# A two-layer attention and MLP kernel: transposes of the LayerNorm output moved from TensorE to the DMA queue, with a reordered start and a split last store

## Chip, cores and metric

The kernel runs on one core of a Trainium2 chip. The metric is device time in microseconds (us) of one execution. All executions used here were fast (within 1.5% of the fastest of the same kernel). "PE" is TensorE, "DVE" VectorE, "ACT" ScalarE, "POOL" GpSimd and "SP" the engine whose queue issues all DMAs here.

## The reference, cut to what matters

```python
# x: 1 x 2048 x 1024, bf16;  H = 32 heads of 32;  window of W = 8 keys, 2 apart;  F = 3584
x = x + attention(layernorm(x), wqkv, wo)      # q.k over 8 earlier rows, softmax, weighted sum of v, @ wo
x = x + gelu(layernorm(x) @ w1 + b1) @ w2 + b2
x = x + attention(layernorm(x), wqkv, wo)      # the same weights a second time
x = x + gelu(layernorm(x) @ w1 + b1) @ w2 + b2
```

Almost all the arithmetic is in four matrix products per layer (wqkv, wo, w1, w2). In the code, the matmuls of wqkv and w1 take both operands with D on partitions, in eight steps of 128 (for wqkv `lhsT=ws[:, kk, dl, :]`, `rhs=xnT[:, kk, :]`). A normalised tile has rows on partitions, so it is transposed before each of wqkv and w1, to bring its columns onto partitions.

## The kernel before

The 2048 rows are cut into 4 chunks of 512 rows, each of 4 tiles of 128. Two layers make 8 chunk steps. A software clock decides where the attention of a later chunk is put between the MLP matmuls of an earlier one, so that DVE works on attention while PE works on the MLP. LN1 is the LayerNorm ahead of the attention, LN2 the one ahead of the MLP. These parts are touched:

```python
def ln_units(xt):
    xnT = xtpool.tile([P, KT, C], BF, name="xnT")
    def a_unit(st):                                  # statistics and normalisation of one 128-row tile
        # ... bn_stats, bn_aggr on DVE into mv
        nc.gpsimd.tensor_scalar(out=rstd, in0=mv[:, 1:2], scalar1=EPS, scalar2=None, op0=ALU.add)
        nc.gpsimd.tensor_tensor(out=rstd, in0=rstd, in1=neghalf, op=ALU.pow)
        xn = xnpool.tile([P, D], BF, name="xn")
        last = nc.vector.tensor_scalar(out=xn, in0=xt[:, st, :], scalar1=mv[:, 0:1], scalar2=rstd, ...)
    def b_unit(st):                                  # transpose of that tile: 8 matmuls against the identity
        xn = xns.pop(st)
        for g in range(2):
            pt = psaux.tile([P, 4, P], F32, name="pa")
            for j in range(4):
                kk = g * 4 + j
                nc.tensor.matmul(pt[:, j, :], lhsT=xn[:, kk * P:(kk + 1) * P], rhs=ident, start=True, stop=True)
            nc.scalar.activation(out=xnT[:, g * 4:(g + 1) * 4, st * P:(st + 1) * P], in_=pt, func=AF.Copy)
# ...
# attention: red() = reduction of q*k products over each head, exp() = softmax,
# bc(0), bc(1) = broadcast of the weights of a head to its lanes: 8 matmuls of 32 rows each, evicted by ACT to attn4,
# pv(dl) = product with v and sum over the window, on DVE, for dl = 0..7
# ...
def store_x(i, xt):                                  # one chunk, 1 MB, in one DMA
    nc.sync.dma_start(out=dst[c * C:(c + 1) * C, :].rearrange("(t p) d -> p t d", p=P), in_=xt)
# ...
# the head: chunk 0 and the projections of chunk 1
xa[0] = ln_all(xts[0])                               # a(st), b(st) for the 4 tiles
us0 = qkv_units(0, xa.pop(0), qks[0])                # q0 k0 q1 k1 ... then v0..v7
# ...
xa[1] = sched_ln1(1, clk.t)
for u in us0[1:]: clk.run(u, T_MM)
sched_att(0, qks.pop(0), 16 * T_MM + 4.5)            # softmax of chunk 0, placed by the clock, after the v units
us1 = qkv_units(1, xa.pop(1), None)
for u in us1[:21]: clk.run(u, T_MM)
run_wo(0, r)                                         # output projection of chunk 0, its LN2
# ... then the loop over 8 chunk steps: W1 and gelu, W2, store, projections of the next chunks
```

## Time and profile before

| | before |
|---|---|
| time, median of 4 executions (lowest to highest) | 1306.25 us (1304.83 to 1306.96) |
| span of the profiled execution | 1304.7 us |
| PE busy | 1272.7 us (98%) |
| first matmul of the first MLP | 135.71 us |
| period of the loop over chunk steps | 158.1 to 158.9 us |
| from the end of the last DVE addition to the end | 5.5 us |

The first lines are from the page of the kernel before: engine totals, then 40 equal slices of the span with busy tenths and the granted PE clock in tenths, then a queue line (packets, MB, share of 16 engines), then two groups of instructions (count, busy us and mean ns, then the idle time before them and what ended it).

```profile
PE 1272.7 (98%) x8031; PEld 826.9 (63%) x8120; DVE 789.1 (60%) x829; ACT 401.7 (31%) x648; POOL 176.7 (14%) x196
...
PE   6998999999999999999999999999999999999998
...
PEclk9998999999999999999999999999999999999999
...
q1 hardware_dynamic: 186832, 201.60, 48.3%
...
L167 ACT ACTIVATE xnT<-pa 128x512 bf16<-128x512 f32 x128 | 69.2, 595 | 421.2 <-PE pa L165 421.1
...
L165 PE MATMUL pa<-ident,xn 128*128 128x128 bf16 x512 | 42.9, 224 | 14.5 <-POOL rstd L152 10.0
```

PE is full from the fifth slice to the last. What it does there must come off PE, or nothing is gained. L165 is the transpose: 512 matmuls, 64 groups of 8.

The busy time of such short matmuls overlaps (512 of 224 ns would be 114.7 us, and the line has 42.9 us), so a group's price is read from the timeline of PE in the kernel before (start us, us, engine, line, operation, count):

```profile
562.65 0.81 PE L289 MATMUL ps<-wt,o 128*128 128x512 bf16 x3
563.30 0.61 PE L165 MATMUL pa<-ident,xn 128*128 128x128 bf16 x8
563.75 3.62 PE L289 MATMUL ps<-wt,o 128*128 128x512 bf16 x15
567.20 0.61 PE L165 MATMUL pa<-ident,xn 128*128 128x128 bf16 x8
```

From the start of a group to the start of what follows is 563.75 - 563.30 = 0.45 us. The period of the loop is read from the chain that ended last, at the long W2 piece of two successive steps (start us, us, what):

```profile
524.26 30.58 PE ps L331 x280
...
682.78 30.57 PE ps L331 x280
```

The head has a gap. In the timeline of PE in the kernel before, these are the output projection after its wait, and the first matmul of the first MLP:

```profile
116.41 1.89 PE L289 MATMUL ps<-wt,o 128*128 128x512 bf16 x4 [3.94 <-DVE o L282]
...
135.71 1.02 PE L307 MATMUL ps<-xnT,wt 128*128 128x512 bf16 x3 [0.78 <-ACT xnT L167]
```

The bracket says that PE had been idle for 3.94 us until DVE delivered o, the result of pv. What the clock did then shows in the windows of the kernel before. Each line has the window, its length, busy us with counts for PE, weight loads, DVE, ACT and POOL, then the granted clock, the DMA share and GB/s:

```profile
111.67:115.08 3.41, 0.80 (x4) 0.18 (x2) 3.41 (x4) 0.00 (x0) 0.00 (x0) 1.00 0.00 0
115.08:118.50 3.42, 2.09 (x5) 0.73 (x6) 2.20 (x5) 0.00 (x0) 0.00 (x0) 0.51 0.00 0
118.50:121.90 3.40, 3.40 (x9) 1.21 (x8) 3.15 (x7) 0.00 (x0) 0.63 (x2) 0.50 0.00 0
```

PE had almost nothing to do for 3.4 us while DVE was busy throughout, and then ran at half clock for 6.8 us. The tail is read from the last DVE instruction in the timeline of the kernel before, which ends at 1299.24 of 1304.7:

```profile
1298.55 0.69 DVE L334 TENSOR_TENSOR xt<-ps,xt 128x512 bf16<-128x512 f32 x1 [5.42 <-PE ps L331]
```

### The profile page before, as it was taken

To read this page: it belongs to the slowest core of one execution; us is meant where nothing else is said; L and a number is where in the kernel's file an instruction comes from. 1 tells how busy PE (TensorE), PEld (TensorE's weight loads), DVE (VectorE), ACT (ScalarE), POOL (GpSimd) and SP (SyncE) were. 2 spreads that over 40 slices of the span, in tenths; PEclk is the share of its full clock that TensorE was granted. 3 is DMA by queue.
4 is the path that set the end of the run, shared out by engine and by line. 5 is a ranking of instruction groups with operands and counts; after the bars stand their busy time and mean duration, and the time that the engine had idled before them with its cause. 6 is when DMAs were issued, how large, how long until landed. Compare 5 with 4: busy or idle time off the path is not lost.

```text
span 1304.7 us, 18295 instructions
## 1 busy us (share of the span) xinstructions
PE 1272.7 (98%) x8031; PEld 826.9 (63%) x8120; DVE 789.1 (60%) x829; ACT 401.7 (31%) x648; POOL 176.7 (14%) x196
## 2 busy tenths in 40 slices
PE   6998999999999999999999999999999999999998
PEld 3564458664686646856478654876548765577477
DVE  5559958894916948188671886528774484843001
ACT  3341441136212362023620345203541035401310
POOL 3002200320004100042000420003200210003000
PEclk9998999999999999999999999999999999999999
DMA  9322554634555345454464445463545435544560
GB/s 296 131 74 114 184 153 134 246 114 148 135 185 195 125 159 155 145 194 170 120 163 159 164 170 167 116 210 114 203 136 170 170 107 184 146 145 157 163 165 33
DMA packets 186912, 202.77 MB, mean 155 GB/s; under 512 B 5456, under 2 KB 152912, under 8 KB 185808
## 3 DMA queue, kind: packets, MB, share of 16 engines
q1 hardware_dynamic: 186832, 201.60, 48.3%
q8 instruction: 63, 1.03, 0.3%
q14 instruction: 17, 0.14, 0.0%
HBM read 193.21 MB, written 8.39 MB: 155 GB/s over the span
## 4 chain that ended last, share of the span: by engine, by line
PE 90%; DVE 4%; DMA 4%; POOL 1%; issue 0%; ACT 0%; SPq 0%; DVEq 0%; ACTq 0%
PE ps L331 30%; PE ps L307 30%; PE ps L189 21%; PE ps L289 6%; PE pa L165 2%; DMA xmid<-xt 2%; DVE prod L279 1%; DMA wt<-in_A_wqkv_dram 1%; DMA xt<-xmid 1%; DVE prod L280 1%; DVE stats L147 1%; DVE prod L211 1%; PE lg L199 1%; DVE prod L281 0%; PE lg L269 0%
## 5 line engine op out<-in xcount | busy, mean ns | idle before, releaser
L331 PE MATMUL ps<-wt,h 128*128 128x256 bf16 x3584 | 399.5, 273 | 0.0
L307 PE MATMUL ps<-xnT,wt 128*128 128x512 bf16 x1752 | 389.3, 379 | 2.9 <-ACT xnT L167 0.8
L331 PEld LDWEIGHTS <-h 128*128 128x128 bf16 x3584 | 348.9, 98 | 42.7 <-issue 1.2
L189 PE MATMUL ps<-xnT,wt 128*128 128x512 bf16 x1503 | 336.4, 380 | 2.6 <-DMA wt<-in_A_wqkv_dram 0.7
L307 PEld LDWEIGHTS <-wt 128*128 128x128 bf16 x1792 | 173.8, 98 | 212.8 <-issue 6.6
L189 PEld LDWEIGHTS <-wt 128*128 128x128 bf16 x1536 | 218.3, 144 | 113.1 <-issue 4.7
L334 DVE TENSOR_TENSOR xt<-ps,xt 128x512 bf16<-128x512 f32 x64 | 44.1, 690 | 312.3 <-PE ps L331 312.3
L310 ACT ACTIVATE h<-ps,b1t 128x512 bf16<-128x512 f32 x224 | 152.8, 689 | 200.9 <-PE ps L307 198.7
L167 ACT ACTIVATE xnT<-pa 128x512 bf16<-128x512 f32 x128 | 69.2, 595 | 421.2 <-PE pa L165 421.1
L279 DVE TENSOR_TENSOR prod<-attn,v 128x4096 bf16<-128x4096 bf16 x64 | 143.8, 2284 | 76.0 <-ACT attn L274 76.0
L211 DVE TENSOR_TENSOR prod<-q,k 128x4096 bf16<-128x4096 bf16 x64 | 151.5, 2394 | 17.0 <-ACT k L190 17.0
L289 PE MATMUL ps<-wt,o 128*128 128x512 bf16 x496 | 116.8, 386 | 5.7 <-DVE o L282 4.9
L151 POOL TENSOR_SCALAR rstd<-mv 128x1 f32<-128x1 f32 x64 | 36.3, 567 | 600.8 <-DVE mv L149 600.0
L218 DVE TENSOR_TENSOR prod<-prod 128x4096 bf16<-128x4096 bf16 x49 | 112.0, 2286 | 0.3
L147 DVE BATCH_NORM_STATS2 stats<-xt 128x6 f32<-128x512 bf16 x128 | 84.2, 676 | 11.3 <-DMA xt<-xmid 5.6
L289 PEld LDWEIGHTS <-o 128*128 128x128 bf16 x512 | 50.0, 99 | 62.6 <-DVE o L282 6.3
L280 DVE TENSOR_TENSOR prod<-prod 128x2048 bf16<-128x2048 bf16 x64 | 75.5, 1216 | 0.0
L317 POOL TENSOR_TENSOR xt<-xt,b2bc 128x1024 bf16<-128x1024 bf16 x32 | 70.0, 2189 | 21.1 <-DVE xn L154 21.1
L190 ACT ACTIVATE q<-ps 128x512 bf16<-128x512 f32 x64 | 38.3, 599 | 78.0 <-PE ps L189 71.2
L190 ACT ACTIVATE v<-ps 128x512 bf16<-128x512 f32 x64 | 38.2, 598 | 72.0 <-PE ps L189 69.3
L190 ACT ACTIVATE k<-ps 128x512 bf16<-128x512 f32 x64 | 38.2, 598 | 69.7 <-PE ps L189 69.7
L165 PE MATMUL pa<-ident,xn 128*128 128x128 bf16 x512 | 42.9, 224 | 14.5 <-POOL rstd L152 10.0
(49 smaller groups left out, 412.9 us busy)
## 6 DMA issues: line engine op xcount, KB each, us to landing
wt<-in_B_w_dram SPq DMA_DIRECT2D x64, 1792.0 KB, 8.1
wt<-in_A_wqkv_dram SPq DMA_DIRECT2D x24, 2048.0 KB, 8.5
wt<-in_A_wo_dram SPq DMA_DIRECT2D x8, 2048.0 KB, 7.7
xmid<-xt SPq DMA_DIRECT2D x4, 1024.0 KB, 10.5
xt<-xmid SPq DMA_DIRECT2D x4, 1024.0 KB, 5.5
out_dram<-xt SPq DMA_DIRECT2D x4, 1024.0 KB, 9.7
xt<-in_A_x_dram SPq DMA_DIRECT2D x3, 1024.0 KB, 7.2
xt<-in_A_x_dram SPq DMA_DIRECT2D x4, 256.0 KB, 3.5
```

What stands on the lines that cost most here:

```text
L147: nc.vector.bn_stats(out=stats[:, hh, :], in_=xt[:, st, hh * 512:(hh + 1) * 512])
L189: nc.tensor.matmul(pt, lhsT=ws[:, kk, dl, :], rhs=xnT[:, kk, :], start=(kk == 0), stop=(kk == KT - 1))
L190: nc.scalar.activation(out=dst[:, dl, off:off + C], in_=pt, func=AF.Copy)
L211: ins = nc.vector.tensor_tensor(out=prod, in0=q8[:, dl, :].unsqueeze(1).to_broadcast([P, W, C]), in1=window(k8, dl), op=ALU.mult)
L218: nc.vector.tensor_tensor(out=self.acc, in0=self.acc, in1=prod, op=ALU.add)
L279: nc.vector.tensor_tensor(out=t, in0=attn4, in1=window(v8, dl), op=ALU.mult)
L280: nc.vector.tensor_tensor(out=t[:, 0:4, :], in0=t[:, 0:4, :], in1=t[:, 4:8, :], op=ALU.add)
L289: nc.tensor.matmul(pt, lhsT=o8[:, dl, st * P:(st + 1) * P], rhs=wt[:, dl, hf * 512:(hf + 1) * 512], start=(dl == 0), stop=(dl == 7))
L307: nc.tensor.matmul(pt, lhsT=wt[:, kk, j * P:(j + 1) * P], rhs=xnT[:, kk, :], start=(kk == 0), stop=(kk == KT - 1))
L310: nc.scalar.activation(out=h, in_=pt, func=AF.Gelu_apprx_tanh, bias=b1t[:, f:f + 1])
L317: nc.gpsimd.tensor_tensor(out=xt[:, st, :], in0=xt[:, st, :], in1=b2bc, op=ALU.add)
L331: nc.tensor.matmul(pt[:, s2, :], lhsT=hs[f][:, st * P:(st + 1) * P], rhs=wt[:, f, :], start=(f == 0), stop=(f == FT - 1))
```

## The change

The intent is fourfold: take the transposes off PE by letting the DMA queue do 56 of 64 (52 in the loop, 4 for chunk 1 in the head); start the first projection earlier and order its units so that weight loads are hidden; run the softmax of chunk 0 directly after its last reduction, with the v units over it, so that DVE starts pv earlier; and store the last chunk in four column blocks, so that only the last quarter is exposed.

```diff
-A_RED, A_EXP, A_BC0, A_BC1, A_PV, A_PVSTEP = 2.0, 8.0, 16.0, 19.5, 23.0, 4.3
+A_RED, A_EXP, A_BC0, A_BC1, A_PV, A_PVSTEP = 2.0, 8.0, 16.0, 21.0, 23.0, 4.3
@@ pools: xnpool bufs 3 -> 5, hpool bufs FT + 2 -> FT
@@ ln_units
+            if act_rstd:                                   # chunk 0 only
+                nc.scalar.activation(out=rstd, in_=mv[:, 1:2], func=AF.Sqrt, bias=epst)
+                nc.vector.reciprocal(out=rstd, in_=rstd)
+        def t_unit():
+            for st in range(ST):
+                nc.sync.dma_start_transpose(out=xnT[:, :, st * P:(st + 1) * P], in_=xns.pop(st))
@@ run_wo and sched_ln1: b(st) on PE only if on_pe, otherwise one t() for the four tiles
@@ head
+    us0 = [us0[n] for n in (0, 2, 4, 1, 6, 3, 8, 5, 10, 7, 12, 9, 14, 11, 13, 15)] + us0[16:]
-    xa[1] = sched_ln1(1, clk.t)
-    for u in us0[1:]:
+    xa[1] = sched_ln1(1, 9.0, False)
+    for u in us0[1:16]:
         clk.run(u, T_MM)
-    sched_att(0, qks.pop(0), 16 * T_MM + 4.5)
+    clk.flush()
+    red, exp, bc, pv = att_units(0, qks.pop(0))
+    red(); exp(); bc(0); bc(1)
+    for u in us0[16:]:
+        clk.run(u, T_MM)
+    for dl in range(8):
+        pv(dl)
-    run_wo(0, r)
+    run_wo(0, r, True)                                     # the first LN2 stays on PE
@@ loop
-            xa[j + 2] = sched_ln1(j + 2, clk.t + 2.0)
+            xa[j + 2] = sched_ln1(j + 2, clk.t + 2.0, False)
-            if early_wo and n == 5:
-                run_wo(j + 1, r)
+            if early_wo and n == 4:
+                run_wo(j + 1, r, False)
+            if j == N - 1 and n % 2 == 1:
+                store_cols(j, xj, n // 2)                  # 256 KB of columns after each pair of W2 units
-        store_x(j, xts.pop(j))
+        if j < N - 1:
+            store_x(j, xj)
# cut: a warm-up of POOL's power function, PE durations in the software clock, signatures
```

## The prediction

> **What bounds it now.** TensorE (PE). The page's busy table gives PE 1272.7 of 1304.7 us (98%), DVE 60%, ACT 31%; the DMA queue takes 48% of its engines' time. From 150 us to the end PE is nearly gapless (stretch table: 25.8 to 26.0 of every 26 us). Of its 32 us of idle about 21 lie before 140 us: 10 before the first matmul, about 3 in 25 to 40, 6 in 105 to 120, where the output projection waits for the last P·V products on DVE. That gap is followed by a granted clock of 0.52 and 0.80 in the stretches from 115 and 120 us, worth about 3 us more. The tail is 5.5 us: last DVE add ends at 1299.2, then the store of a 1 MB tile.

> **Removed.** 56 of 64 transpose groups of 8 matmuls leave PE for the DMA queue (instruction order: 13 chunks' LayerNorms inside the main loop, one in the head; two stay on PE). A group holds PE for 0.45 us (timeline 563.30 to 563.75). 52 x 0.45 = 23.4 us in the loop, plus about 1.5 us of interruptions (0.3 us waiting for xn, four-matmul pieces inside W2). All of it is critical: the loop period 158.2 us (chain of waits, W2 at 524.26 and 682.78) should fall to 154 to 155. The 112 ACT evictions that go (67 us) gain nothing.

> **Head.** Softmax of chunk 0 now runs right after the last head reduction, with 44 V matmuls (about 9.7 us) over it, so the attention weights should be in place near 68 us instead of 82.4. The 34.2 us of P·V on DVE then end near 102, when PE, at its 0.219 us per matmul, just arrives at the output projection (about 103). The projection should end near 118.5 instead of 128.5, without the clock drop: 10 us, one transposed chunk included. The square root on ACT saves about 1 us before the first projection; three q tiles first hide the wait for k weights (landed 18.2).

> **Tail.** The last store shrinks to a quarter: about 2.5 us.

> **Added.** 56 DMA transposes of 256 KB, 14.7 MB on 202.8. [...] Results are needed 25 us or more after their inputs are ready, and the three-deep weight ring leaves a 8.1 us load some 16 us of slack (12.1 us per piece), so even 5 us each should hide. The sync queue is in order: a transpose waiting for xn delays weight loads behind it. In the issue order four LN1 transposes stand before the fourth W1 load; xn should be ready before that load's buffer is.

> **Sum.** 23.4 + 1.5 + 10 + 2.5 = 37 us: 1269 us, range 1257 to 1288. Faster by over 2% 0.80, within 2% 0.15, slower 0.05.

> **Right if:** transposing matmuls fall from 512 to 64; loop period near 154.5; PE gapless over 100 to 120 us at full clock; projection of chunk 0 starting near 103; PE busy near 1247.

> **Wrong if:** transposes take over 5 us, or fill the DMA engines, or block the sync queue: then W1 or xnT waits "<-DMA" appear on PE, at the fourth W1 piece or the first W1 matmul of a chunk, and DVE waits for a free xn buffer. Or if the head becomes bound by DVE (27 us of products and LN1 against 27 us of PE), with PE waiting for reductions near 50 us.

## The result, and the profile after

| | before | after |
|---|---|---|
| time, median (lowest to highest) | 1306.8 us (1304.68 to 1309.49, 13 executions) | 1266.84 us (1264.85 to 1268.38, 8 executions) |
| ratio, 95% interval | | 0.9693 (0.9684 to 0.9703) |
| profiled span | 1304.7 us | 1267.0 us |
| PE busy | 1272.7 us | 1244.5 us |
| first matmul of the first MLP | 135.71 us | 127.43 us |
| period of the loop | 158.1 to 158.9 us | 154.03 us |
| tail after the last DVE addition | 5.5 us | 3.1 us |

A ratio here is the mean time of one kernel's fast runs over that of the other's in the same rounds, so it is not quite the ratio of the medians that are quoted. The difference of 3.1% makes it faster. All outputs agreed with the reference.

The lines of the page after that answer to those shown of before:

```profile
PE 1244.5 (98%) x7589; PEld 803.2 (63%) x7672; DVE 786.3 (62%) x834; ACT 344.8 (27%) x541; POOL 151.6 (12%) x190
...
PEclk9989999999999999999999999999999999999999
...
q1 hardware_dynamic: 247552, 216.29, 57.8%
```

The transposes left on PE, from the groups of the kernel after:

```profile
L182 ACT ACTIVATE xnT<-pa 128x512 bf16<-128x512 f32 x16 | 8.7, 595 | 11.6 <-PE pa L180 11.6
L180 PE MATMUL pa<-ident,xn 128*128 128x128 bf16 x64 | 6.7, 261 | 9.6 <-DVE xn L169 9.0 <-ACT xnT L182 0.4 <-DVE mv L160 0.3
```

The DMA transposes, from the view of tile xnT of the kernel after. The first line has the time that the issuing queue spent on one (ns, min/median/max), the second the time from issue to landing:

```profile
L186 SPq DMA_TRANSPOSE xnT<-xn x56: 1232/1318/6108, 30.9 to 1145.5; - x56
...
DMA to landing us min/median/max: 3.0/4.3/9.2
```

The chain of the kernel after, at the W2 block of two successive steps. The block is now 448 matmuls without interruption:

```profile
487.09 48.91 PE ps L343 x448
...
641.12 48.91 PE ps L343 x448
```

All waits of PE from 130 to 1262 us in the kernel after. There is one, and it is not for a DMA:

```profile
PE ps L301 <- DVE o L294: 1.4, 1, 1.4
```

The head, in the timeline of PE of the kernel after: the output projection follows the projections of chunk 1 at once.

```profile
97.77 8.15 PE L201 MATMUL ps<-xnT,wt 128*128 128x512 bf16 x36
105.75 1.46 PE L301 MATMUL ps<-wt,o 128*128 128x512 bf16 x6
...
127.43 0.81 PE L319 MATMUL ps<-xnT,wt 128*128 128x512 bf16 x3 [0.73 <-ACT xnT L182]
```

Windows of the kernel after, columns as above:

```profile
60.68:64.09 3.41, 2.42 (x11) 0.83 (x10) 0.71 (x1) 2.14 (x5) 0.00 (x0) 1.00 0.00 0
64.09:67.50 3.41, 3.41 (x8) 1.11 (x8) 1.25 (x1) 2.48 (x5) 0.00 (x0) 0.50 0.00 0
67.50:70.92 3.42, 3.20 (x8) 1.32 (x8) 3.42 (x3) 0.60 (x1) 0.00 (x0) 0.50 0.34 93
```

The half clock is still there in this execution. It has moved from 115 us to 64 us, to where the broadcasts of chunk 0 now stand, although PE was busy for 2.42 of the 3.41 us ahead of it. The last DVE instruction in the timeline of the kernel after ends at 1263.89 of 1267.0:

```profile
1263.20 0.69 DVE L346 TENSOR_TENSOR xt<-ps,xt 128x512 bf16<-128x512 f32 x1 [5.42 <-PE ps L343]
```

Splitting both profiled spans at the first MLP matmul and at the end of the last DVE addition gives where the 37.7 us between the two profiles came from. Head: 135.71 - 127.43 = 8.3 us. Loop: (1299.24 - 135.71) - (1263.89 - 127.43) = 27.1 us. Tail: 5.46 - 3.11 = 2.3 us.

### The profile page after: what moved, and what is told of

The parts are those of the page before. It is cut to its first block, busy times and chain, and to the rows that moved or that the text cites. A ratio compares the mean times of both kernels' runs of the same rounds, so it can differ in the third digit from the quotient of the medians.

```text
span 1267.0 us, 17391 instructions
## 1 busy us (share of the span) xinstructions
PE 1244.5 (98%) x7589; PEld 803.2 (63%) x7672; DVE 786.3 (62%) x834; ACT 344.8 (27%) x541; POOL 151.6 (12%) x190
## 3 DMA queue, kind: packets, MB, share of 16 engines
q1 hardware_dynamic: 247552, 216.29, 57.8%
## 4 chain that ended last, share of the span: by engine, by line
PE 92%; DVE 5%; ACT 1%; issue 1%; DMA 0%; POOL 0%; SPq 0%; DVEq 0%; ACTq 0%
PE ps L319 30%; PE ps L343 28%; PE ps L201 24%; PE ps L301 9%; DVE prod L291 1%; DVE prod L223 1%; DVE prod L292 1%; PE lg L281 0%; DVE prod L293 0%; DVE stats L158 0%; PE lg L211 0%; DMA xt<-in_A_x_dram 0%; DVE xt L346 0%; ACT xnT L182 0%; PE pa L180 0%
## 5 line engine op out<-in xcount | busy, mean ns | idle before, releaser
L343 PE MATMUL ps<-wt,h 128*128 128x256 bf16 x3584 | 393.1, 273 | 0.0
L201 PEld LDWEIGHTS <-wt 128*128 128x128 bf16 x1536 | 220.0, 144 | 118.5 <-issue 10.1
L346 DVE TENSOR_TENSOR xt<-ps,xt 128x512 bf16<-128x512 f32 x64 | 44.2, 690 | 301.7 <-PE ps L343 301.7
L301 PE MATMUL ps<-wt,o 128*128 128x512 bf16 x497 | 111.5, 379 | 2.2 <-DVE o L294 1.4
L166 POOL TENSOR_SCALAR rstd<-mv 128x1 f32<-128x1 f32 x60 | 23.6, 393 | 495.3 <-DVE mv L160 491.2
L304 DVE TENSOR_TENSOR xt<-ps,xt 128x512 bf16<-128x512 f32 x64 | 43.0, 672 | 16.3 <-PE ps L301 15.8
L196 POOL COPY v<-v 128x112 bf16<-128x112 bf16 x6 | 13.6, 2269 | 313.3 <-DVE prod L291 313.3
```

Of the source, the lines that this page charges most:

```text
L201: nc.tensor.matmul(pt, lhsT=ws[:, kk, dl, :], rhs=xnT[:, kk, :], start=(kk == 0), stop=(kk == KT - 1))
L301: nc.tensor.matmul(pt, lhsT=o8[:, dl, st * P:(st + 1) * P], rhs=wt[:, dl, hf * 512:(hf + 1) * 512], start=(dl == 0), stop=(dl == 7))
L343: nc.tensor.matmul(pt[:, s2, :], lhsT=hs[f][:, st * P:(st + 1) * P], rhs=wt[:, f, :], start=(f == 0), stop=(f == FT - 1))
```

## The experiments

The theory under test is the prediction's: the gain is the sum of three independent parts, PE time of the transposes, an earlier softmax in the head, and a smaller last store, and the DMA transposes are hidden. The rivals are: that the DMA transposes cost time that a better placement would give back (contention, queue order); that the head's part came from something else; and, once the half clock at 64 us was seen, several ideas of what sets it off. Each edit below is against the changed kernel unless said otherwise. Kernels that ran on the same chip share the runs of the kernel before. The kernel before had medians between 1306.5 and 1307.5 us in those rounds.

### Undo the loop's transposes

```diff
-            xa[j + 2] = sched_ln1(j + 2, clk.t + 2.0, False)
+            xa[j + 2] = sched_ln1(j + 2, clk.t + 2.0, True)
-                run_wo(j + 1, r, False)          # both places
+                run_wo(j + 1, r, True)
```

> The changed kernel with the 52 LayerNorm tiles of the main loop transposed on TensorE again; the head, the tail and the buffer counts stay changed. Theory (the middle gain is TensorE time given back): the loop period goes from 154.0 back to about 158 us, the transposing matmuls from 64 to 480, the total to about 1267 + 27 = 1294 us, ratio to before about 0.990. Rival (the gain comes from the head and from more xn buffers, the transposes only moved): within 5 us of 1267.

Measured: 1294.7 us (1291.55 to 1295.61), ratio to before 0.9907 (0.9891 to 0.9922). That is 27.9 us more than the changed kernel. The W2 pieces of the chain stand at 515.25, 673.79 and 832.10, so the loop period is back at 158.3 to 158.5 us. What follows: the loop's transposes are worth about 27 us, and the rest of the change about 12 us.

### Only the DMA transposes, on the kernel before

```diff
# against the kernel before
+        def t_unit():
+            for st in range(ST):
+                nc.sync.dma_start_transpose(out=xnT[:, :, st * P:(st + 1) * P], in_=xns.pop(st))
# used for the 52 tiles in the loop; xnpool bufs 5, hpool bufs FT; head and tail as before
```

> The kernel before with one part of the change alone: the 52 LayerNorm tiles of the main loop go through DMA transposes (with five xn and 28 h buffers), head and tail stay old. Theory (parts add up; the loop's part is TensorE time): loop period 154.0 us, total 1306.5 - 27 = 1279.5. Rival (the loop gains only because the head no longer leaves DVE and the DMA queue late): gain under 15 us.

Measured: 1278.21 us (1278.05 to 1278.9), ratio 0.9778 (0.9761 to 0.9796). The loop period is 154.03 us, as the W2 blocks in the chain of this run show:

```profile
494.20 48.91 PE ps L335 x448
...
648.23 48.91 PE ps L335 x448
```

What follows: done alone, the transposes bring 29 us; taken away, they cost 28 us. The parts add up to about 1 us, so they hardly depend on each other. Per group the loop's 27.1 us between the two profiles are 27.1 / 52 = 0.52 us, not the 0.45 us of the timeline. A group seems to cost a little at its edges too, in the matmuls around it; that was not measured by itself.

### Double the DMA transposes

```diff
+                xn = xns.pop(st)
+                nc.sync.dma_start_transpose(out=xnT[:, :, st * P:(st + 1) * P], in_=xn)
+                scr = scrp.tile([P, KT, P], BF, name="scr")          # read by nobody
+                nc.sync.dma_start_transpose(out=scr, in_=xn)
```

> The changed kernel with every DMA transpose issued twice, the second time into a scratch tile that nobody reads (112 transposes in place of 56). Theory (their 1.8 us of all DMA engines each, 4.3 us to landing, are hidden in the slack of the weight ring): DMA share of the queue from 58% to about 67%, total no more than 1 us longer, TensorE without waits for weights. Rival (the DMA queue is near its limit and the transposes already delay weight loads a little): TensorE waits for weights or for xnT appear in the loop, and the total grows by 5 us or more.

Measured: 1267.79 us (1264.75 to 1267.93), ratio 0.9696 (0.9683 to 0.971), the same as the changed kernel. Its queue line, and all waits of PE from 130 to 1262 us in this run:

```profile
q1 hardware_dynamic: 306688, 230.98, 64.8%
```

```profile
PE ps L305 <- DVE o L298: 1.4, 1, 1.4
```

What follows: 56 transposes more, and PE waits for none in the loop. The rival that they cost time there through contention or the queue's order is refuted. The cost in DMA time can be worked out. Going from before to after, (57.8% of 1267.0 - 48.3% of 1304.7) / 56 = 1.8 us of all 16 engines for each transpose of 256 KB, or 144 GB/s. Going from after to this run, (64.8% of 1266.2 - 57.8% of 1267.0) / 56 = 1.6 us, or 166 GB/s. That is more than other transfers take: the whole queue before, with 201.6 MB in 48.3% of 1304.7 us, moved 320 GB/s, so 256 KB in 0.8 us. It is hidden all the same.

### The last LN2 that stayed on PE, by DMA too

```diff
-    run_wo(0, r, True)
+    run_wo(0, r, False)
```

> The changed kernel with the one LayerNorm that it still transposes on TensorE before the first MLP also sent through DMA transposes. There the first MLP matmul follows the last normalized tile by some 3 us. Theory (a DMA transpose costs latency, 3.0 to 9.2 us to landing, which only slack hides): TensorE saves 4 x 0.45 = 1.8 us and then waits 3 to 6 us for xnT; total 2 to 4 us longer, with a wait of the first MLP matmul for a DMA. Rival (latency is hidden here as well): 1.8 us shorter.

Measured: 1273.51 us (1270.08 to 1274.99), ratio 0.9737 (0.9716 to 0.9758), which is 6.7 us slower than the changed kernel, more than the 2 to 4 us expected. The timeline of this run, PE and the queue, at the start of the first MLP:

```profile
121.73 2.54 PE L201 MATMUL ps<-xnT,wt 128*128 128x512 bf16 x11
124.68 1.24 SPq L186 DMA_TRANSPOSE xnT<-xn  x1
126.01 0.98 SPq L72 DMA_DIRECT2D wt<-in_B_w_dram  x1
129.47 1.87 PE L319 MATMUL ps<-xnT,wt 128*128 128x512 bf16 x4 [5.20 <-issue]
```

The last transpose was issued at 124.68 and PE stood still until 129.47. The label "issue" names no releaser, but PE's next work needs all four tiles of xnT, and the DMAs landed 3.0 to 9.3 us after issue, 4.1 us in the median. A half clock from 128.0 to 134.8 us came on top, which the expectation had left out. What follows: the DMA transpose is cheap only because the loop leaves time for its latency. Where the result is wanted at once, it costs 5 us of waiting, so this group is rightly left on PE.

### The softmax of chunk 0 back at its old place

```diff
-    for u in us0[1:16]:
+    for u in us0[1:]:
         clk.run(u, T_MM)
-    clk.flush()
-    red, exp, bc, pv = att_units(0, qks.pop(0))
-    red(); exp(); bc(0); bc(1)
-    ...                                            # v units, pv
+    sched_att(0, qks.pop(0), 16 * T_MM + 4.5)
# cut: a flush of the software clock before run_wo
```

> The changed kernel with only the place of chunk 0's softmax undone: broadcasts of the attention weights after 72 and 96 more projection matmuls, as before. Theory (the head's 8 us come from starting P.V earlier): attention weights near 80 us, P.V ends near 115, TensorE waits some 4 us in front of the output projection, total about 8 us more: 1275 us. Rival (the head's gain is the square root on ScalarE and the order of the q and k tiles): no change, 1267 within 1.5 us.

Measured: 1272.32 us (1271.73 to 1272.88), ratio 0.9739 (0.9726 to 0.9753), 5.5 us slower than the changed kernel against some 8 expected. The timeline of PE in this run:

```profile
103.00 3.63 PE L301 MATMUL ps<-wt,o 128*128 128x512 bf16 x16 [1.78 <-DVE o L294]
111.55 6.39 PE L301 MATMUL ps<-wt,o 128*128 128x512 bf16 x20 [4.92 <-DVE o L294]
```

What follows: the waits for o are back, pv starts at 77.5 us instead of 66.2, and a half clock follows at 111.7 to 115.1 us, while the one at 64 us is gone. The first MLP matmul stands at 131.06 us. Against the changed kernel's profile that is 3.6 us later, against a profile of the same head without a half clock (the next run, 123.94 us) 7.1 us. The mechanism is as predicted; the expected size left out that the changed kernel itself often pays for a half clock.

### The whole last store

```diff
-            if j == N - 1 and n % 2 == 1:
-                store_cols(j, xj, n // 2)
-        if j < N - 1:
-            store_x(j, xj)
+        store_x(j, xj)
```

> The changed kernel with the last chunk stored in one 1 MB piece. Theory: time from the last add to the end goes from 3.1 back to about 5.5 us, total 2.3 us more (1269.2). Rival: the four stores of 512-byte rows disturb the last weight loads, so undoing them gains: total no longer than 1267.

Measured: 1268.79 us (1267.23 to 1270.52), ratio 0.9713 (0.9698 to 0.9727). In its profile the last addition ends at 1260.40 of 1265.8 us, a tail of 5.4 us against 3.1 us:

```profile
1259.71 0.69 DVE L346 TENSOR_TENSOR xt<-ps,xt 128x512 bf16<-128x512 f32 x1 [5.42 <-PE ps L343]
```

What follows: the split store is worth 2.3 us at the end, seen in the profile; in the medians it is 2.0 us, with intervals that overlap. By chance this profile had no half clock in the head: the output projection begins at 102.3 us and the first MLP matmul at 123.94 us, against 105.75 and 127.43 us after. So the same code runs with the half clock or without it, 3.5 us apart.

### Broadcasts after more projections

To close the 0.70 us gap before the broadcasts, they were put behind the v units and the first unit of chunk 1, by an order dependency on PE.

```diff
-    red(); exp(); bc(0); bc(1)
+    red(); exp()
     # v units
+    bc(0, last)                     # after the last v unit
+    last = us1[0]()
+    bc(1, last)                     # after the first q unit of chunk 1
```

> The changed kernel with the two broadcasts of chunk 0's attention weights put behind all 64 V matmuls and behind 8 more, so that TensorE does not wait for the softmax and does not run single broadcasts that wait for evictions. The stretch from 60 to 63 us, where the changed kernel's TensorE is busy 0.84, 0.46 and 0.71 of each us, is followed there by 6.8 us at clock 0.5 in some runs (3.4 us lost) and not in others. Theory (the low-activity spell makes the drop): no drop in the profile, about 1 us gained from the waits in every run and 3.4 more in the runs that had the drop: median near 1264, highest run below 1267. Rival (the drop comes by itself, or from the broadcasts' narrow matmuls whatever stands around them): drop and spread stay, median within 1 us of 1266.8.

Measured: 1270.5 us (1269.28 to 1271.28), ratio 0.9718 (0.97 to 0.9736): slower than the changed kernel, where some 3 us less were expected. The timeline of PE in this run:

```profile
103.41 1.01 PE L201 MATMUL ps<-xnT,wt 128*128 128x512 bf16 x2 [4.22 <-ACT v L202]
```

What follows: there was no half clock at 64 us, but pv began at 68.3 us instead of 66.2, and PE met the end of pv instead. It waited for a psum buffer, which waited for ACT's eviction of v, which waited for POOL's copy of the halo of v, which has to wait until the last pv has read the old one (by the waits of this run 4.2 us of PE for ACT's v, 9.8 us of ACT for POOL's v and 47.7 us of POOL for DVE's prod). A half clock followed at 102.2 us, and all 4 executions had a mean clock of 0.997. Against the profile of the changed kernel, which also has 6.8 us at half clock, the span is 1269.2 - 1267.0 = 2.2 us longer, about the 2.1 us by which pv began later. The head is bound by the chain on DVE, so this delay of pv was paid in full.

### A warm-up of PE

```diff
+    pw = psaux.tile([P, 4, P], F32, name="pa")
+    for n in range(64):
+        nc.tensor.matmul(pw[:, n % 4, :], lhsT=ident, rhs=ident, start=True, stop=True)
```

> The changed kernel with 64 matmuls of the identity with itself, whose result nobody reads, at the very start, while TensorE waits for the first LayerNorm (it idles to 9.0 us). In the changed kernel a group of 8 transposes takes 1.07 us there against 0.45 later, and a 512-column matmul 0.43 against 0.22, until 16.2 us. Theory (TensorE starts at half rate and needs several us of work first, though the clock column says 1.0): groups take about 0.5 us, first projection starts near 13.4 in place of 14.1 and runs at 0.22, total about 1.5 us shorter. Rival (the first matmuls are slow for the loads that run at the same time): no change in them.

Measured: 1270.19 us (1266.94 to 1271.66), ratio 0.9713 (0.9691 to 0.9734). No gain, and confounded: the extra work made the scheduler put the statistics of chunk 1 ahead of the first products of q and k, which then began at 26.96 us instead of 22.96. The first lines of PE's timeline in this run:

```profile
1.62 5.60 PE L106 MATMUL pa<-ident 128*128 128x128 bf16 x64 [1.62 <-POOL ident L102]
8.53 0.62 PE L183 MATMUL pa<-ident,xn 128*128 128x128 bf16 x8 [1.31 <-DVE xn L172]
10.70 0.87 PE L183 MATMUL pa<-ident,xn 128*128 128x128 bf16 x8 [1.55 <-ACT xnT L185]
```

The first group of transposes took 0.62 us here and 1.04 us in the changed kernel, with the same loads in flight (a DMA share of 1.04 at 8 to 10 us here, 1.05 at 9 to 16 us there), so it is PE's state and not the loads that slows the first matmuls. The 0.87 us of the second group are no slow clock: its matmuls start 0.055 us apart (0.107 us in the changed kernel), in two halves of four with 0.32 us between them. The windows of this run show that the full clock lasted to 12.37 us and was then lost:

```profile
5.54:8.95 3.41, 2.10 (x37) 1.93 (x35) 3.41 (x11) 0.85 (x3) 0.45 (x2) 1.00 1.03 392
8.95:12.37 3.42, 1.47 (x19) 1.02 (x17) 1.98 (x7) 2.53 (x7) 0.00 (x0) 1.00 1.05 393
12.37:15.78 3.41, 3.24 (x17) 1.75 (x16) 0.00 (x0) 2.20 (x4) 0.00 (x0) 0.50 1.05 387
```

The first projection began at 14.11 us against 14.06. What follows: the warm-up did warm PE, but the chain of transposes that waits for DVE and ACT ran no shorter for it, and its thin work let the clock fall again before the first projection. This run has three half clocks, which is of use below.

### The old start

```diff
-    xnT0, a0, b0, _ = ln_units(xts[0], act_rstd=True)
+    xnT0, a0, b0, _ = ln_units(xts[0], act_rstd=False)
-    us0 = [us0[n] for n in (0, 2, 4, 1, 6, 3, 8, 5, 10, 7, 12, 9, 14, 11, 13, 15)] + us0[16:]
```

> The changed kernel with the start undone: square root back on POOL as a power, q and k tiles strictly in turn again. Theory (these two are worth about 1 us at the first projection): first projection at about 15.1 in place of 14.1 us, TensorE waits for the k weights at 18.2 as before; the head ends 1 to 2 us later, total 1268 to 1269. Rival (the P.V chain swallows it): same as the changed kernel within 0.5 us.

Measured: 1266.6 us (1265.88 to 1267.64), ratio 0.9694 (0.968 to 0.9707). The first projection begins at 15.23 us instead of 14.06. None of its 5 executions had a mean clock below 0.999, and the profiled one shows no half clock in the head; the spans were 1264.2 to 1265.9 us, while executions of the changed kernel at clock 1.000 took 1263.1 to 1263.7 us. By the medians the rival's expectation came true: no difference from the changed kernel. What follows: by the executions at full clock the square root on ACT is worth about 1 us, which the missing half clock hides in the medians (this rests on few executions). No wait for weights of k appeared, so this run does not show that the new order of q and k units gains anything.

### Broadcasts pinned inside the last v unit, and the control

```diff
+        plan = {1: [(0, 0), (0, 1), (0, 2), (0, 3)], 4: [(1, 0)], 6: [(1, 1)], 7: [(1, 2)]}
+        for kk in range(KT):                       # the 8 matmuls of the last v unit
+            for wh, sb in plan.get(kk, []):
+                prev = follow(piece(wh, sb), prev) # one broadcast, in this order on PE
+            prev = follow(nc.tensor.matmul(pt, lhsT=ws[:, kk, 7, :], rhs=xnT[:, kk, :], ...), prev)
+        follow(piece(1, 3), prev)
```

> The changed kernel with the eight broadcast matmuls of chunk 0 pinned into the last V unit: after 57 V matmuls, then after 60, 62, 63 and 64. P.V should start as early as in the changed kernel (about 66 us; in the run with the broadcasts behind everything it started at 68.3 and TensorE waited 4.2 us for the v halo copy, which waits for the last P.V), but TensorE should have no gap in front of the broadcasts. Theory (two things bind the head: the P.V chain's start, and the clock drop that a thin spell of TensorE work triggers in some runs): no drop in any run, P.V still done by 100 us, median 1263.3 to 1264.5 and a spread under 1.5 us. Rival (the drop is not set off by the gap): spread of 1264.8 to 1268.4 as before.

The control, the changed kernel unaltered:

> The changed kernel itself on the same chip as the two runs beside it, as a control: median 1266.8, times between 1264.8 and 1268.4, the longer ones with a mean granted clock of 0.997 and the shorter with 1.000.

Measured: pinned 1265.92 us (1264.69 to 1266.29), ratio 0.9684 (0.9671 to 0.9698); control 1268.15 us (1267.28 to 1268.32), ratio 0.9702 (0.9688 to 0.9715). The pinned kernel had mean clocks of 0.999 to 1.000 in 4 executions and no half clock in its profile, the control 0.997 in 3 of 4. What follows: with PE kept dense around the broadcasts the half clock was not seen, which 4 executions alone cannot prove to be the cause, and the kernel is 2.2 us faster than its control. Their executions do not overlap, the intervals of the ratios just do. The control happened to have the half clock more often than the changed kernel in the first call; against that median the gain is 0.9 us. It is not faster by the whole 3.4 us, because PE now waits for 1.09 us at 101.2 us for the eviction of v: the chain of pv binds again.

### The pinned kernel with a longer gap

This is the rival's test: if a thin spell of PE sets off the half clock, a gap of 2 us at the same place should bring it every time. The edit is against the pinned kernel and puts the broadcasts one unit earlier, so that PE arrives before the weights are ready.

```diff
-        plan = {1: [(0, 0), (0, 1), (0, 2), (0, 3)], 4: [(1, 0)], 6: [(1, 1)], 7: [(1, 2)]}
+        plan = {0: [(0, 0), (0, 1), (0, 2), (0, 3)], 3: [(1, 0)], 5: [(1, 1)], 6: [(1, 2)], 7: [(1, 3)]}
-    # inside the eighth v unit
+    # inside the seventh v unit
```

> The kernel with the pinned broadcasts, but the first four are pinned before V matmul 49 instead of after 57, so that TensorE waits about 2 us for the softmax (nothing else removed or added). Theory (a thin 3.4 us spell sets off 6.8 us at half clock): the drop now comes in most or all executions (mean clock 0.997), and the total is about 2 us of waiting plus 3.4 us of lost clock above the pinned version's 1265.9, less about 1 us that the pinned version waited later: 1269.5 to 1271. Rival (the drop comes with chance and the gap is innocent): at most 2 us above 1265.9, and about half of the executions at clock 0.997.

Measured: 1265.83 us (1265.73 to 1268.72), ratio 0.9694 (0.9681 to 0.9707). The expectation failed. Two windows of this run:

```profile
58.80:60.80 2.00, 0.03 (x1) 0.01 (x1) 1.84 (x2) 0.60 (x1) 0.00 (x0) 1.00 0.00 0
60.80:70.90 10.10, 10.07 (x45) 5.59 (x46) 5.61 (x4) 6.31 (x12) 0.00 (x0) 1.00 0.27 91
```

The gap of 2 us is there, and the clock stays full after it. Only 1 of 5 executions had a mean clock of 0.997, and it took 1267.0 us of span; the others took 1264.0 to 1265.2 us at clock 1.000. What follows: a gap of 2 us does not reliably set off the half clock, and costs nothing itself, because pv binds the head (the output projection begins at 102.8 us and the MLP at 124.5 us, as in the pinned kernel; pv even began 0.8 us earlier, at 65.3 us, with the earlier broadcasts).

### What the half clocks of all profiles have in common

The grid can be had for profiles without a half clock too. Each begins with PE at half pace: in the kernel after, matmuls of 512 columns start 0.427 us apart until 16.31 us and 0.216 us apart from there. (The record starts with this first change, so the column of the clock shows 1.00 before it.) From 16.31 to the half clock at 64.09 us it is 14.0 times 3.413 us, so this change lies on the grid as well. In the kernel before it is 29.0 times, from 16.19 to 115.17 us.

Here is what stood in the grid window ahead of each half clock, and in the windows of the other profiles that came nearest to it. "Whole" counts the matmuls on the whole array by their pace (0.216 us for 512 columns, 0.056 us for 128), "partial" those on 32 of its 128 rows or columns (the broadcasts and the reductions) in the same way:

| run | window, us | PE busy in it, of 3.41 us | whole, us | partial, us | half clock for |
|---|---|---|---|---|---|
| before | 111.76 to 115.17 | 0.71 | 0.54 | 0 | 6.8 us |
| after | 60.68 to 64.09 | 2.42 | 0.65 | 1.43 | 6.8 us |
| loop's transposes undone | 59.43 to 62.84 | 2.42 | 0.93 | 1.29 | 6.8 us |
| double transposes | 59.70 to 63.12 | 2.43 | 0.84 | 1.29 | 6.8 us |
| control | 59.44 to 62.86 | 2.43 | 0.93 | 1.29 | 6.8 us |
| only DMA transposes | 113.22 to 116.63 | 0.50 | 0.49 | 0 | 3.4 us |
| late softmax | 108.24 to 111.66 | 0.11 | 0.11 | 0 | 3.4 us |
| broadcasts later | 98.77 to 102.19 | 0.42 | 0.26 | 0 | 6.8 us |
| warm-up, first | 8.95 to 12.37 | 1.47 | 0.82 | 0 | 3.4 us |
| warm-up, second | 26.02 to 29.43 | 1.29 | 0.98 | 0.57 | 3.4 us |
| warm-up, third | 63.57 to 66.98 | 2.42 | 0.68 | 1.39 | 6.8 us |
| first LN2 by DMA, first | 59.76 to 63.17 | 2.42 | 0.93 | 1.29 | 6.8 us |
| first LN2 by DMA, second | 124.60 to 128.02 | 0.00 | 0 | 0 | 6.8 us |
| whole last store | 59.54 to 62.95 | 2.43 | 0.99 | 1.29 | none |
| longer gap | 59.73 to 63.15 | 2.32 | 1.08 | 1.29 | none |
| old start | 61.39 to 64.80 | 3.12 | 1.20 | 0.86 | none |
| pinned broadcasts | 61.10 to 64.51 | 3.36 | 1.63 | 1.43 | none |

The busy time does not tell the two kinds apart: 2.43 us stand in both. The whole matmuls do. A window with up to about 1 us of them was followed by a half clock, and one with more was not. This fits every window at full clock in the 14 profiles, up to the last matmuls (there 1.01 us were followed by it and 1.28 us were not). The partial matmuls count for little: were the control's 1.29 us of broadcasts worth more than about 0.3 of whole ones, its window would have come above those 1.28 us. The control and the run with the whole last store, which has the same head, differ by 0.2 us in where the grid lies: the window begins 1.23 us before the first broadcast in the one and 1.42 us in the other. First the control:

```profile
59.44:62.86 3.42, 2.43 (x12) 0.81 (x10) 1.08 (x1) 1.78 (x4) 0.00 (x0) 1.00 0.00 0
62.86:69.68 6.82, 6.82 (x16) 2.27 (x16) 4.05 (x2) 3.44 (x7) 0.00 (x0) 0.50 0.08 14
```

Then the run with the whole last store:

```profile
59.54:62.95 3.41, 2.43 (x12) 0.80 (x10) 1.24 (x2) 1.65 (x5) 0.00 (x0) 1.00 0.00 0
62.95:66.36 3.41, 3.41 (x14) 1.83 (x14) 0.94 (x1) 3.35 (x7) 0.00 (x0) 1.00 0.00 0
```

So the changed kernel gets a half clock when one grid window covers most of its thin spell, and not when a boundary splits the spell, as at 61.39 us in the run with the old start. By the trace of the whole last store, a window that begins anywhere in some 1.55 us of the 3.41 us would hold less than 0.99 us: an estimate of 45%, if the grid falls anywhere alike. 6 of 13 executions of the changed kernel had a mean clock of 0.997, which is what 6.8 us at half speed make of 1267 us. Shifted over the pinned kernel's trace, no window near the broadcasts holds less than 1.45 us, and 0 of 4 executions had the half clock. For the longer gap the same estimate gives 45% again, and it was seen in 1 of 5. The old start has the thin spell of the changed kernel, and 0 of 5 would then be a chance of about 5%; the grid is on record for its profiled execution alone. The reading was made after the runs and no experiment set where the grid lies, so it is inferred from these traces and was not tested on a new one.

## Why the prediction was right or wrong, point by point

The predicted time was 1269 us with a range of 1257 to 1288; the median was 1266.84 us. The total was right, and so was the mechanism of each large part, with the sizes and one step off.

- **PE bounds the kernel, and what leaves PE comes off whole: right, 2.2 us too small.** The term "23.4 + 1.5" was 24.9 us, and the loop gave 27.1 us. A group of transposes was worth 0.52 us and not 0.45 us plus 1.5 us in all for interruptions. Undoing it cost 27.9 us, doing it alone brought 29 us. The period was foreseen at 154 to 155 us and came to 154.03.
- **The DMA transposes are hidden: right.** They took 1.6 to 1.8 us of all DMA engines each, and landed 4.3 us after issue. Doubling them cost nothing that shows (0.95 us in the medians, with intervals that overlap). The queue did stand before transposes until DVE had their input, as the prediction feared, up to 12.8 us at a time (two transposes then went out from 164.10 us, and the next weight load behind them at 167.82 us), and PE waited for no weights all the same. The prediction had found a slack of some 16 us, and had left room for 5 us each; the slowest landed after 9.2 us, hidden as well.
- **The head, 10 us: the mechanism right, the step "without the clock drop" wrong.** The waits of PE for o in the head, 0.9 and 3.9 us, fell to none, and putting the softmax back cost 5.5 us. But the half clock did not always go. All executions of the kernel before that have it on record had a mean clock of 0.996 to 0.998; of the changed kernel 6 of 13 had 0.997, and in the profile it had moved from 115 us to 64 us, where the broadcasts now stand. It cost 3.5 us. The prediction looked for a gap at the old place and did not ask whether the new order leaves a thin spell elsewhere. The head gave 8.3 us in a profile with the half clock; in the profile without it, 135.71 - 123.94 = 11.8 us. The 10 us lie between. They include the transposes of chunk 1, 4 x 0.45 = 1.8 us by the prediction's price, which no run took away alone.
- **The square root on ACT, about 1 us: right**, 15.23 us against 14.06 us for the first projection, and about 1 us of span. The order of q and k units, which was to hide a wait for k weights, showed no effect of its own: that wait did not come back without it.
- **The tail, 2.5 us: right**, 2.3 us.
- **The checks:** transposing matmuls fell from 512 to 64, PE busy is 1244.5 us (1247 foreseen), PE waits for no DMA in the loop, and the output projection begins at 105.75 us with a half clock and at 102.3 us without (103 foreseen). The full clock over 100 to 120 us was met, but for the wrong reason to count on: it was lost earlier instead.

The sum of parts in the profiles is 8.3 + 27.1 + 2.3 = 37.7 us, against 37 us predicted: the loop gave 2 us more, and the head, with its half clock, 2 us less. That the two cancel is luck. The medians are 40.0 us apart: the profile of the changed kernel is one with the half clock, and about half of its executions have none.

## What to carry to other kernels

Where PE was full and gapless, as in this loop, work taken off PE shortened the kernel by all its PE time, though it cost more elsewhere, because the stage had slack for the new latency: the same DMA transpose was free in the loop and cost 5 us where its result was wanted at once. In a head bound by a chain of latencies, find the chain (here pv on DVE and the halo copy behind it) before closing gaps on another engine, since here a gap of 2 us on PE cost nothing and a delay of 2 us of pv was paid in full. After reordering, look for thin spells of PE at the new place, counting whole-array matmuls and not busy time (here 2.42 us of PE work in 3.41 us, with no gap over 0.70 us and only 0.65 us of whole matmuls, were followed by a half clock), and judge a half clock by several executions, because the same code had a mean clock of 0.997 in 6 of 13 and of 0.999 to 1.000 in the others.
